# Rearranging the first stage of a transformer block on one core: conditioning vector in rows, a later gate load, fourteen extra products and a share of the normalisation on GpSimd

## The chip, the cores and the metric

The kernel runs on one core of a Trainium2 chip. A core has TensorE (matrix products; the profile's PE, with PEld for the loading of the stationary operand), VectorE (DVE), ScalarE (ACT), GpSimd (POOL), and SyncE (SP), which issues all DMAs of this kernel. Each engine works through its own instructions in order; semaphores tie the engines together. The metric is the device time of one execution in microseconds (us), as a median of several runs.

## The reference

The input x has 2048 tokens of 1024 channels. A vector c of 1024 numbers goes through silu and a 1024 x 6144 matrix and gives six modulation vectors.

```
mod = silu(c) @ w_mod              -> sa, ca, ga, sb, cb, gb
h = layernorm(x) * (1 + ca) + sa
x = x + ga * attention(h)          # 32 heads of 32, four segments of 512 tokens,
                                   # masked softmax inside a segment plus a running memory,
                                   # mixed by g = sigmoid(beta), one g per head
h = layernorm(x) * (1 + cb) + sb
x = x + gb * mixer(layernorm(h))   # W2 gelu(W1 .) across the tokens, 3584 hidden
```

## The kernel before, in words

**Stages.** First comes an opening of about 70 us: it loads x, makes the first two modulation vectors, normalises segment 0 and projects it. Attention over eight groups of four heads and four segments follows until about 1000 us, then the output projection and the two products of the token mixer, which TensorE fills until the end.

**Precision.** Operands of the large products are kept as two parts, a rounded one ("hi", made by a cast) and the rest ("lo", made by a subtraction); three products hi·hi, hi·lo and lo·hi stand for one. `split` makes both parts: for weights and for the pages of segment 0 ScalarE casts and VectorE subtracts; for the pages of segment 1 VectorE casts, and the subtraction goes to VectorE for odd and to GpSimd for even chunks. A "page" `h{seg}_{ct}` is one chunk of 128 channels by 512 tokens of the modulated, normalised input of a segment. Chunk ct's scale and shift (`saca`) come from two tiles `wm` of the modulation matrix, each multiplied by silu(c) and summed on VectorE (L285).

**The opening, step by step.** c arrives as 128 partitions x 8 (`csb`), silu is made on it, VectorE spreads it (`bc`), TensorE transposes that eight times, and ScalarE copies it out as `scb`, silu(c) on every partition. `norm_tiles` takes the statistics of a set of token tiles on VectorE, makes one over the deviation with Ln and Exp on ScalarE and four short VectorE steps, and then normalises each tile of 128 x 1024 with one ScalarE instruction (L222). `h_chunk` transposes the chunk of four tiles on TensorE (`hps`), applies scale and shift on ScalarE into `h32` (a ring of three buffers) and splits the result. `first_chunk` adds the chunk's products for head groups 0 and 1 (`nps` for keys and values at L182, `qps` for queries at L190). Then segment 1 goes the same way (its tiles are x4 to x7), and its pages feed the third item of the attention stage.

**Gate.** `gate` is sigmoid(beta), loaded by a DMA that reads the same 128 bytes for all 128 partitions. GpSimd multiplies it into eight masks (`bdg`, one product at L318 and one small copy at L321 for each head group), which the memory update of each group needs; the first such update is on VectorE at L429.

**Who sets the order.** The program is written as a stream of instructions. A planner at the end (`Order`) estimates what each instruction costs, walks the program forward and backward in a few passes, and pins the resulting order on every engine. TensorE's instructions count double before `COLD` (28000 ns of the planner's time). A GpSimd product of 128 elements a partition counts 551 ns in its table of costs (520 with a margin of 6%), a small copy 121 ns. These are the planner's figures, not measured ones.

Of the kernel before, what the change touches and what calls it, by code (L numbers as in the profile page):

```python
# [9 lines left out]
F32 = mybir.dt.float32  # L10
# [4 lines left out]
ALU = mybir.AluOpType  # L15
# [5 lines left out]
P = 128  # L21
# [23 lines left out]
def attention_and_mlp(ctx, tc, x, wq, wkv, wo, beta, w1, b1, w2, b2, c, wm_a, wm_b, out):  # L45
# [49 lines left out]
    G.memset(eps, EPS)  # L95

    csb = acst.tile([P, 2, NK], F32, name="csb")
    SY.dma_start(csb[:, 0], c)
    A.activation(csb[:, 1], csb[:, 0], AF.Exp, scale=-1.0)
    V.tensor_scalar_add(csb[:, 1], csb[:, 1], 1.0)  # L100
    V.reciprocal(csb[:, 1], csb[:, 1])
    sc = const.tile([P, NK], F32, name="sc")
    V.tensor_mul(sc, csb[:, 0], csb[:, 1])
# [102 lines left out]
    def norm_tiles(pool, ts):  # L206
        n = len(ts)
        mv = pool.tile([P, n, 4], F32, tag="mvs", bufs=2, name="mvs")
        for i, t in enumerate(ts):
            st = const.tile([P, 2, 6], F32, tag="st", bufs=4, name="st")  # L210
            for j in range(2):
                V.bn_stats(st[:, j], t[:, 512 * j:512 * j + 512])
            V.bn_aggr(mv[:, i, 0:2], st)
        m, v, r, e = (mv[:, :, j] for j in range(4))
        A.activation(r, v, AF.Ln, bias=eps)
        A.activation(r, r, AF.Exp, scale=-0.5)
        V.scalar_tensor_tensor(e, v, EPS, r, op0=ALU.add, op1=ALU.mult)
        V.scalar_tensor_tensor(e, e, -0.5, r, op0=ALU.mult, op1=ALU.mult)
        V.scalar_tensor_tensor(r, e, 1.5, r, op0=ALU.add, op1=ALU.mult)
        V.scalar_tensor_tensor(e, m, -1.0, r, op0=ALU.mult, op1=ALU.mult)  # L220
        for i, t in enumerate(ts):
            A.activation(t, t, AF.Identity, scale=mv[:, i, 2:3], bias=mv[:, i, 3:4])  # L222

    def h_chunk(pool, xs, seg, ct):
        ps = bank("s2", 2, f"hps{seg}_{ct}")
# [35 lines left out]
    bc = s1p.tile([P, NK, P], F32, name="bc")  # L261
    V.tensor_copy(bc, sc.unsqueeze(2).to_broadcast([P, NK, P]))
    for i in range(2):
        ps = bank("pj", 2, f"scps{i}")
        for j in range(4):
            T.transpose(ps[:, 128 * j:128 * j + 128], bc[:, 4 * i + j], ident)
        A.copy(scb[:, 512 * i:512 * i + 512], ps)
    first = [[bank("pj", 2, "nps0_0"), bank("pj", 2, "nps0_1"), bank("s1", 2, "qps0")],
             [bank("pv", 1, "nps1_0"), bank("ms", 1, "nps1_1"), bank("s1", 2, "qps1")]]
# [11 lines left out]
    for ct in range(NK):  # L281
        for part in range(2):
            wm = s1p.tile([P, D], F32, tag="wm", bufs=11, name=f"wm{ct}_{part}")
            SY.dma_start(wm, wm_a[part, ct])
            V.scalar_tensor_tensor(wm, wm, 1.0, scb, op0=ALU.mult, op1=ALU.mult, accum_out=saca[:, ct, part:part + 1])  # L285
        for kind, part, g in parts.get(ct, ()):
            split_part(g, kind, part, fetch_part(g, kind, part))
        V.tensor_scalar_add(saca[:, ct, 1:2], saca[:, ct, 1:2], 1.0)
        h_chunk(s1p, xs[0], 0, ct)
        if ct:  # L290
            for g in range(2):
                first_chunk(g, ct - 1)
# [3 lines left out]
    norm_tiles(s2p, xs[1])  # L296
    for ct in range(NK):
        h_chunk(s2p, xs[1], 1, ct)
    gate = top.tile([P, 3, H], F32, name="gate")
    SY.dma_start(gate[:, 0], bass.AP(tensor=beta.tensor, offset=beta.offset, ap=[[0, P], [1, H]]))  # L300
    A.activation(gate[:, 1], gate[:, 0], AF.Exp, scale=-1.0)
    V.tensor_scalar_add(gate[:, 1], gate[:, 1], 1.0)
    V.reciprocal(gate[:, 0], gate[:, 1])
    V.tensor_scalar(gate[:, 1], gate[:, 0], -1.0, 1.0, op0=ALU.mult, op1=ALU.add)
# [9 lines left out]
    skt = [[q.tile([98, 2, L], F32R, name=f"sk{i}_{h}") for h in range(4)] for i, q in enumerate(sk_)]  # L314
    for sk in skt[0] + skt[1]:
        G.memset(sk[96:98, 1].bitcast(F32), 1.0)
    for g in range(NG):
        G.tensor_tensor(bdg[:, g, 0:128].rearrange("p (h e) -> p h e", h=4),  # L318
                        bd[:, 0:128].rearrange("p (h e) -> p h e", h=4),
                        gate[:, 0, 4 * g:4 * g + 4].unsqueeze(2).to_broadcast([P, 4, 32]), op=ALU.mult)  # L320
        G.tensor_copy(bdg[:, g, 128:132], bd[:, 128:132])  # L321
# [635 lines left out]
LATEB = 3000.0  # L957
HOLD = 1000.0
EARLY = 60000.0
STAY = 3000.0  # L960
SLACK = 1.06
DMA_SPREAD = 7000.0
# [115 lines left out]
class Order:  # L1078
# [182 lines left out]
    def forward(self, key):  # L1261
# [44 lines left out]
                add(i)  # L1306
        while len(seq) < n:
            t, e, i = self.pick(free, heap, future, key)
            x = self.X[i]
            if x.opcode == "DMACopy" and size_of(x.outs[0]) > BULK and link - t - ISSUED > BACKLOG:  # L1310
                heapq.heappush(future[e], (link - ISSUED - BACKLOG, i))
# [159 lines left out]
```

## Time and profile before

| | |
|---|---|
| median of 3 runs | 2207.83 us (2205.8 to 2208.32) |
| the profiled execution | 2210.61 us, its span 2208.9 us |
| TensorE busy | 2162.7 us (98%) |
| VectorE, ScalarE, GpSimd busy | 1732.7, 1097.1, 725.7 us |
| TensorE idle in the first 20 us | 16 us |

The span runs from the first to the last instruction of the profiled execution. Busy times add up instructions; a busy TensorE is not one at full rate, so the length of single products is worth reading too.

### The profile page before, as it was taken

What the parts mean: (1) busy time and instruction counts of PE and PEld (TensorE: products, weight loads), DVE (VectorE), ACT (ScalarE), POOL (GpSimd) and SP (SyncE); (2) the same over time, 40 slices, a digit from 0 to 9 for tenths busy, and PEclk for the clock granted to TensorE, in tenths of its full rate; (3) what the DMA queues carried; (4) which work ended last, traced back from release to release, by engine and by line L of the source; (5) the groups of instructions that cost most, each with busy time, mean ns of one, the idle gap of its engine ahead of it and who ended that gap; (6) DMA issues with size and microseconds to landing.
All of it is one profiled execution on the core that took longest, in us unless ns stands there. A gap on an engine that the chain in (4) does not pass through costs nothing.

```text
span 2208.9 us, 38272 instructions
## 1 busy us (share of the span) xinstructions
PE 2162.7 (98%) x13738; PEld 1876.5 (85%) x13738; DVE 1732.7 (78%) x3818; ACT 1097.1 (50%) x2008; POOL 725.7 (33%) x827
## 2 busy tenths in 40 slices
PE   6999999999999999989999999999999999999999
PEld 6899998989988999878878888888888888888887
DVE  8777777867787756678997555898889787878787
ACT  5688787566666665653443333633334242424232
POOL 3376676476777755551001000043321000000000
PEclk9999999999999999999999999999999999999999
DMA  9666676796777644664467555775549241414134
GB/s 370 189 204 189 192 223 196 244 288 201 224 213 235 181 135 107 191 211 157 139 238 277 191 194 197 276 278 200 201 175 337 86 157 58 149 53 148 58 124 152
DMA packets 174897, 421.74 MB, mean 191 GB/s; under 512 B 17492, under 2 KB 71796, under 8 KB 165748
## 3 DMA queue, kind: packets, MB, share of 16 engines
q1 hardware_dynamic: 174708, 419.30, 57.9%
q8 instruction: 109, 1.79, 0.3%
q14 instruction: 80, 0.66, 0.1%
HBM read 242.00 MB, written 126.37 MB: 167 GB/s over the span
## 4 chain that ended last, share of the span: by engine, by line
PE 83%; DVE 7%; POOL 2%; DMA 2%; ACT 2%; issue 1%; SPq 0%; DVEq 0%; POOLq 0%; ACTq 0%
PE mx L787 46%; PE nps L182 13%; PE qps L190 6%; PE po L688 4%; PE pv L498 4%; POOL ph L484 2%; PE a L469 1%; PE sz L445 1%; PE sx L445 1%; PE rd L417 1%; PE up L427 1%; PE a L472 1%; PE a L475 1%; PE sy L445 1%; PE ops L513 1%
## 5 line engine op out<-in xcount | busy, mean ns | idle before, releaser
L787 PE MATMUL mx<-bU,sp 128*128 128x512 f32 x2352 | 533.7, 389 | 0.9 <-DVE bU L116 0.9
L787 PEld LDWEIGHTS mx<-bU,sp 128*128 128x128 f32 x2352 | 441.3, 188 | 93.2 <-DVE bU L116 1.3
L113 ACT CAST sp<-wr 128x384 fp32r<-128x384 f32 (+2 forms) x408 | 218.4, 545 | 474.3 <-PE mx L787 386.8
L182 PE MATMUL nps<-wv,h 128*128 128x256 f32 x3072 | 444.8, 284 | 0.8 <-POOL h L116 0.6
L787 PE MATMUL mx<-bA,sp 128*128 128x512 f32 x1764 | 433.5, 389 | 1.6 <-ACT cc L792 0.7
L484 POOL TENSOR_TENSOR ph<-p,ph 128x640 f16<-128x640 f32 x256 | 385.3, 1524 | 110.1 <-ACT ph L482 109.0
L182 PEld LDWEIGHTS nps<-wv,h 128*128 128x128 f32 x3072 | 405.6, 189 | 7.0 <-POOL h L116 0.8
L787 PEld LDWEIGHTS mx<-bA,sp 128*128 128x128 f32 x1764 | 330.4, 188 | 72.7 <-ACT cc L792 1.3
L116 DVE TENSOR_TENSOR sp<-wr,sp 128x384 fp32r<-128x384 f32 (+2 forms) x408 | 260.4, 646 | 60.6 <-ACT sp L113 60.1
L794 DVE TENSOR_TENSOR ac<-mx,ac 128x512 f32<-128x512 f32 x280 | 190.7, 688 | 94.6 <-PE mx L787 93.4
L190 PE MATMUL qps<-h,wq 128*128 128x512 f32 x768 | 198.7, 400 | 0.1
L482 ACT CAST ph<-p 128x1280 f16<-128x1280 f32 x128 | 161.4, 1261 | 52.5 <-POOL p L480 51.5
L688 PE MATMUL po<-wo,ots 128*128 128x512 f32 x768 | 182.4, 392 | 0.5 <-ACT mv L125 0.5
L480 POOL TENSOR_SCALAR_AFFINE_SELECT p<-p 128x256 f32<-128x256 f32 x256 | 117.6, 469 | 188.8 <-ACT p L477 94.8
L688 PEld LDWEIGHTS po<-wo,ots 128*128 128x128 f32 x768 | 143.6, 189 | 29.8 <-ACT mv L125 0.9
L190 PEld LDWEIGHTS qps<-h,wq 128*128 128x128 f32 x768 | 140.8, 190 | 29.7 <-PE sz L445 0.5
L787 PE MATMUL mx<-bB,sp 128*128 128x512 f32 x588 | 165.9, 389 | 0.0
L446 DVE CUSTOM_DVE_ANT_0 sx<-sx,mask 128x128 f32<-128x128 f32 (+1 forms) x256 | 110.9, 434 | 69.6 <-PE sx L445 68.9
L659 POOL TENSOR_TENSOR tu<-cc 128x512 f32<-128x512 f32 x14 | 19.1, 1364 | 399.5 <-DVE cc L923 372.1
L787 PEld LDWEIGHTS mx<-bB,sp 128*128 128x128 f32 x588 | 110.4, 188 | 23.0
L498 PE MATMUL pv<-vp,ph 128*128 128x97 bf16 (+1 forms) x2560 | 117.1, 200 | 1.7 <-DVE am L505 1.0
L794 DVE TENSOR_TENSOR cc<-mx,cc 128x512 f32<-128x512 f32 x140 | 95.2, 684 | 25.6 <-PE mx L787 22.0
(179 smaller groups left out, 3258.3 us busy)
## 6 DMA issues: line engine op xcount, KB each, us to landing
sk<-sg SPq DMA_DIRECT2D x384, 128.0 KB
wr<-in_w_dram SPq DMA_DIRECT2D x28, 1024.0 KB
wr<-in_w_dram SPq DMA_DIRECT2D x32, 768.0 KB
bstu<-ucd SPq DMA_DIRECT2D x28, 768.0 KB
wv<-wsp SPq DMA_DIRECT2D x36, 512.0 KB
wsp<-wv SPq DMA_DIRECT2D x32, 512.0 KB
rawm<-in_wm_b_dram SPq DMA_DIRECT2D x32, 512.0 KB
pcd<-cc SPq DMA_DIRECT2D x14, 1024.0 KB
```

The costliest lines, as they stand in the source:

```text
L113: A.copy(hi, src)
L116: lo_eng.tensor_tensor(lo, src, hi.bitcast(F32), op=ALU.subtract)
L182: T.matmul(ps[:, aa], h[:, j, 128 * tt:128 * tt + 128], wt[:, i, o:o + 256], start=(n == 0), stop=(n >= 6 * NK - 2), skip_group_check=True)
L190: T.matmul(ps, wt[:, i, o:o + 128], h[:, j], start=(k + n == 0), stop=(3 * k + n == 3 * NK - 1))
L446: V.tensor_tensor_reduce(o, o, mask[:, 384 - 128 * i:], 1.0, -3.0e38, op0=ALU.add, op1=ALU.max, accum_out=mx[:, h % 2, i:i + 1])
L480: G.affine_select(w, w, pattern=[[0, 2], [1, 128]], compare_op=ALU.is_ge, fill=0.0, base=0, channel_multiplier=-1)
L482: A.copy(ph[:, 0], p32)
L484: G.tensor_tensor(ph[:, 1, c], p32[:, c], ph[:, 0, c], op=ALU.subtract)
L498: T.matmul(pv[:, i, 0:w], ph[:, part, o:o + 128], d["vp"][:, j, h, 0:w], start=(n == 0), stop=(n == 19), skip_group_check=True)
L688: T.matmul(ps, os_[:, i, P * ct:P * ct + P], wop[ct, nh][:, j], start=(n == 0), stop=(n == 3 * NK - 1))
L787: T.matmul(ps, ops[q][:, i, P * k:P * k + P], b[:, j], start=(m == 0 and first), stop=(m == 3 * nk - 1), skip_group_check=True)
L794: V.tensor_tensor(d, ps, d, op=ALU.add)
```

## The change

The edits, in the order of the program:

- **c in rows.** c arrives as 8 partitions x 128 (`cr`). silu is made there, and eight products with a selection matrix (`sel`, made by GpSimd) spread it over the partitions, in place of the VectorE copy and eight transposes.
- **Gate later.** The gate's load and its four short steps move from before segment 1's pages to after them in the program, into the pool `late`; the load leaves the start of SP's queue.
- **Extra products.** Fourteen products of 128 x 512 read the first hi weights and write a PSUM bank that is cleared when its first real product starts. Their results are not used.
- **Norms on GpSimd.** In `norm_tiles` every second tile is normalised by GpSimd.
- **Planner.** During the first 30000 ns of its own time the planner may leave VectorE idle for up to 200 ns for an instruction that is due earlier by more than 200.

```diff
-    csb = acst.tile([P, 2, NK], F32, name="csb")   # and its DMA, exp, add, reciprocal, product
+    cr = s1p.tile([NK, 2, P], F32, name="cr")
+    SY.dma_start(cr[:, 0], c)
...
-            T.transpose(ps[:, 128 * j:128 * j + 128], bc[:, 4 * i + j], ident)
+            T.matmul(ps[:, 128 * j:128 * j + 128], sel[:, 4 * i + j], cr[:, 0], start=True, stop=True)
...
         for i, t in enumerate(ts):
-            A.activation(t, t, AF.Identity, scale=mv[:, i, 2:3], bias=mv[:, i, 3:4])
+            if i % 2:
+                G.tensor_scalar(t, t, mv[:, i, 2:3], mv[:, i, 3:4], op0=ALU.mult, op1=ALU.add)
+            else:
+                A.activation(t, t, AF.Identity, scale=mv[:, i, 2:3], bias=mv[:, i, 3:4])
...
+        for pg, n in (((W[0, 0]["v", 0], 8), (W[0, 0]["q", 0], 6)) if ct == 0 else ()):
+            for _ in range(n):
+                T.matmul(first[1][1], pg[:, 0, 0:128], pg[:, 0], start=True, stop=True)
...
-    gate = top.tile([P, 3, H], F32, name="gate")    # its DMA and steps, before the attention pools open
+    gate = b.tile([P, 3, H], F32, name="gate")      # the same lines, after them
...
+            soon = WAIT.get(e, 0.0) if t < SOON else 0.0      # WAIT: DVE 200, Activation 0; SOON 30000
+            if soon and future[e] and future[e][0][0] <= t + soon:
+                near = [(key[j], r, j) for r, j in future[e] if r <= t + soon]
+                k, r, j = min(near)
+                if k < key[i] - EAGER and r < t + self.C[i][0]:      # EAGER 200
+                    heapq.heappush(heap[e], (key[i], i))
+                    free[e] = r
+                    continue
```

Since the planner works from the whole program, every engine's order changes in the opening and, in small swaps, through the first quarter of TensorE's instructions; behind that the orders are the same. Three places matter below. Line numbers of the changed kernel differ from those of before.

TensorE at the start, before; `scps` is the spread silu(c), `hps_0` to `hps_2` the transposes of segment 0's first chunks, `nps_0` the first real product:

```order
L266 MATMUL scps_150<-ident,bc 128x128 x4
L227 MATMUL hps_0_219<-ident,x_134 128x128
L227 MATMUL hps_1_252<-ident,x_134 128x128
L227 MATMUL hps_0_219<-ident,x_136 128x128
L227 MATMUL hps_1_252<-ident,x_136 128x128
```

The same place in the changed kernel (L293 are the extra products):

```order
L269 MATMUL scps_151<-cr,sel 128x128 x4
L293 MATMUL nps_1_161<-wv_0_0_0_205 128x512 x8
L223 MATMUL hps_0_234<-ident,x_128 128x128
L223 MATMUL hps_0_234<-ident,x_130 128x128
L223 MATMUL hps_1_267<-ident,x_128 128x128
L223 MATMUL hps_1_267<-ident,x_130 128x128
L293 MATMUL nps_1_161<-wq_0_0_0_213 128x512 x2
```

The extra products now stand ahead of and between the transposes; four more follow before `hps_2`.

VectorE around the first lo part of a page (`h_0`), before; `saca` is a chunk's scale and shift:

```order
L285 SCALAR_TENSOR_TENSOR wm_0_292,saca<-wm_0_292,scb 128x1024
L288 TENSOR_SCALAR saca<-saca 128x1
L303 RECIPROCAL gate<-gate 128x32
L285 SCALAR_TENSOR_TENSOR wm_1_295,saca<-wm_1_295,scb 128x1024
L116 TENSOR_TENSOR h_0_226<-h_0_0_224,h_0_226 128x512
L288 TENSOR_SCALAR saca<-saca 128x1
L116 TENSOR_TENSOR h_1_259<-h_0_1_257,h_1_259 128x512
```

And in the changed kernel:

```order
L294 TENSOR_SCALAR saca<-saca 128x1
L109 TENSOR_TENSOR wv_1_0_0_252<-rawv_0_250,wv_1_0_0_252 128x512
L288 SCALAR_TENSOR_TENSOR wm_0_307,saca<-wm_0_307,scb 128x1024
L288 SCALAR_TENSOR_TENSOR wm_1_310,saca<-wm_1_310,scb 128x1024
L109 TENSOR_TENSOR h_0_241<-h_0_0_239,h_0_241 128x512
L294 TENSOR_SCALAR saca<-saca 128x1
L109 TENSOR_TENSOR h_1_274<-h_0_1_272,h_1_274 128x512
```

The first lo part still comes behind the same six `wm` sums; the gate's reciprocal has left, and one weight split (`wv_1`) has moved ahead of it.

GpSimd where segment 1's pages are made (`h_0`, `h_2`, `h_4`, `h_6` are the lo parts of the even pages), before; the masks `bdg` stand far ahead of this place:

```order
L316 MEMSET sk_2_760 2x512
L116 TENSOR_TENSOR h_0_662<-h_1_0_660,h_0_662 128x512
L116 TENSOR_TENSOR h_2_682<-h_1_2_680,h_2_682 128x512
L116 TENSOR_TENSOR h_4_702<-h_1_4_700,h_4_702 128x512
L354 MEMSET v_1_838 128x4x4
L116 TENSOR_TENSOR h_6_722<-h_1_6_720,h_6_722 128x512
```

And in the changed kernel:

```order
L216 TENSOR_SCALAR x_637<-x_637,mvs 128x1024
L216 TENSOR_SCALAR x_641<-x_641,mvs 128x1024
L323 TENSOR_TENSOR bdg<-bd,gate 128x128 x2
L109 TENSOR_TENSOR h_0_677<-h_1_0_675,h_0_677 128x512
L326 COPY bdg<-bd 128x4 x2
L323 TENSOR_TENSOR bdg<-bd,gate 128x128
L326 COPY bdg<-bd 128x4
L323 TENSOR_TENSOR bdg<-bd,gate 128x128
L326 COPY bdg<-bd 128x4
L323 TENSOR_TENSOR bdg<-bd,gate 128x128
L109 TENSOR_TENSOR h_2_697<-h_1_2_695,h_2_697 128x512
```

Two norms and all eight mask pairs now share GpSimd's queue with the four lo parts; one pair stands between `h_2` and `h_4`, and the rest of the eight stand ahead of `h_6`.

More of the change, by code (lines that the diff above doesn't have):

```diff
@@ L97, in attention_and_mlp @@
     csb = acst.tile([P, 2, NK], F32, name="csb")
[L98 to L103, printed above, removed]
     saca = acst.tile([P, NK, 2], F32, name="saca")
@@ L208, in norm_tiles @@
         mv = pool.tile([P, n, 4], F32, tag="mvs", bufs=2, name="mvs")
+        m, v, r, e = (mv[:, :, j] for j in range(4))
         for i, t in enumerate(ts):
@@ L213, in norm_tiles @@
             V.bn_aggr(mv[:, i, 0:2], st)
-        m, v, r, e = (mv[:, :, j] for j in range(4))
         A.activation(r, v, AF.Ln, bias=eps)
@@ L260, in attention_and_mlp @@
     xs = {0: [load_x(s1p, tt) for tt in range(4)]}
-    bc = s1p.tile([P, NK, P], F32, name="bc")
-    V.tensor_copy(bc, sc.unsqueeze(2).to_broadcast([P, NK, P]))
+    sel = s1p.tile([NK, NK, P], F32, name="sel")
+    G.memset(sel, 1.0)
+    G.affine_select(sel, sel, pattern=[[-1, NK], [0, P]], compare_op=ALU.is_equal, fill=0.0, base=0, channel_multiplier=1)
+    cr = s1p.tile([NK, 2, P], F32, name="cr")
+    SY.dma_start(cr[:, 0], c)
+    A.activation(cr[:, 1], cr[:, 0], AF.Exp, scale=-1.0)
+    V.tensor_scalar_add(cr[:, 1], cr[:, 1], 1.0)
+    V.reciprocal(cr[:, 1], cr[:, 1])
+    V.tensor_mul(cr[:, 0], cr[:, 0], cr[:, 1])
     for i in range(2):
@@ L298, in attention_and_mlp @@
         h_chunk(s2p, xs[1], 1, ct)
-    gate = top.tile([P, 3, H], F32, name="gate")
[L300 to L304, printed above, removed]
     left.__exit__(None, None, None)
@@ L316, in attention_and_mlp @@
         G.memset(sk[96:98, 1].bitcast(F32), 1.0)
+    gate = b.tile([P, 3, H], F32, name="gate")
+    SY.dma_start(gate[:, 0], bass.AP(tensor=beta.tensor, offset=beta.offset, ap=[[0, P], [1, H]]))
+    A.activation(gate[:, 1], gate[:, 0], AF.Exp, scale=-1.0)
+    V.tensor_scalar_add(gate[:, 1], gate[:, 1], 1.0)
+    V.reciprocal(gate[:, 0], gate[:, 1])
+    V.tensor_scalar(gate[:, 1], gate[:, 0], -1.0, 1.0, op0=ALU.mult, op1=ALU.add)
     for g in range(NG):
@@ L959 @@
 EARLY = 60000.0
+EAGER = 200.0
+WD, WA = 200.0, 0.0
+SOON = 30000.0
+WAIT = {"DVE": WD, "Activation": WA}
 STAY = 3000.0
@@ L1454 @@
         "b2": f("B_b2").reshape(NT, P).T,
-        "c": f("c").reshape(NK, P).T,
+        "c": f("c").reshape(NK, P),
         "wm_a": wm[:, :2 * D].T.reshape(2, NK, P, D),
```

## The prediction

> **What bounds the kernel now.** I read the page first, then busy time by stretch, then the timelines of TensorE, VectorE and GpSimd through the first 75 us.
>
> ```profile
> span 2208.9 us, 38272 instructions
> PE 2162.7 (98%) x13738; PEld 1876.5 (85%) x13738; DVE 1732.7 (78%) x3818; ACT 1097.1 (50%) x2008; POOL 725.7 (33%) x827
> ...
> PE 83%; DVE 7%; POOL 2%; DMA 2%; ACT 2%; issue 1%; SPq 0%; DVEq 0%; POOLq 0%; ACTq 0%
> ...
> core 0: us, PE busy (x) PEld busy (x) DVE busy (x) ACT busy (x) POOL busy (x), PEclk, DMA share, GB/s
> 0.00:10.00 10.00, 1.94 (x8) 1.57 (x8) 3.99 (x10) 3.17 (x6) 2.47 (x19) 1.00 0.68 230
> 10.00:20.00 10.00, 2.07 (x6) 0.87 (x6) 9.36 (x25) 6.89 (x11) 0.00 (x0) 1.00 1.03 415
> 20.00:30.00 10.00, 8.94 (x43) 7.97 (x44) 10.00 (x20) 7.45 (x13) 7.02 (x9) 1.00 1.02 409
> 30.00:40.00 10.00, 10.00 (x75) 9.35 (x74) 10.00 (x20) 3.83 (x6) 7.91 (x8) 1.00 1.03 408
> ```
>
> TensorE is busy for 98% of the span, so only what shortens its idle or slow time counts, and most of that lies in the first 22 us. There VectorE is the full engine (9.36 of 10 us, then all of it). The profiled execution took 2210.61 us, 1.7 more than its span and 2.8 more than the median, 2207.83. I work out a difference and add it to the median.
>
> TensorE's timeline, start and duration first:
>
> ```profile
> 6.30 1.94 PE L266 MATMUL scps<-ident,bc 128*128 128x128 f32 x8 [6.30 <-DVE bc L262]
> ...
> 25.05 1.91 PE L182 MATMUL nps<-wv,h 128*128 128x256 f32 x8
> ...
> 28.24 1.53 PE L182 MATMUL nps<-wv,h 128*128 128x256 f32 x12
> ...
> 71.92 0.74 PE L182 MATMUL nps<-wv,h 128*128 128x256 f32 x4 [0.63 <-POOL h L116]
> ```
>
> Eight products of 256 columns took 1.91 us at 25 us, twelve took 1.53 at 28: 0.24 against 0.13 each. So TensorE ran at half rate until about 27.5 us, although the granted clock of every stretch reads 1.00. From there it worked without a gap until 71.3 us, where it waited 0.63 us for GpSimd to finish page `h_6` of segment 1. These are the two places the change touches.
>
> **c in rows.** TensorE's spread takes 1.94 us now; if a product here costs two passes of a transpose, 3.9. The VectorE copy goes. All of it ends before anyone needs it:
>
> ```profile
> 8.28 0.59 ACT L267 COPY scb<-scps 128x512 f32<-128x512 f32 x1 [0.27 <-PE scps L266]
> ...
> 10.57 1.29 DVE L212 BATCH_NORM_STATS2 st<-x 128x6 f32<-128x512 f32 x2 [1.58 <-DMA x<-in_x_dram]
> ...
> 15.13 1.22 DVE L285 SCALAR_TENSOR_TENSOR wm<-wm,scb 128x1024 f32<-128x1024 f32 x1
> ```
>
> `scb` is ready at 8.9 us and first used at 15.13, so 6 us cover it. Ln and Exp stand behind those copies on ScalarE; a spread 2 us longer makes the first statistics wait until about 11, which uses up what an earlier x tile could give. Price 0.
>
> **The gate's load** leaves SP's queue at the start. While it and c came in, the rate fell:
>
> ```profile
> GB/s 0 0 115 224 374 363 284 115 161 181 302 383 421 421 426 410 415 426 426 421 404 404 426 393 415 426 382 415 426 393 415 415 415 404 404 415 404 404 421 399
> ```
>
> Each figure covers 0.75 us. Against 415, the eight figures from 374 to 383 lack 0.87 MB, about 2.1 us of the stream. VectorE waited 1.58 us for an x tile. Bounds: nothing, to 1.6 us earlier on VectorE. I take none, because of the norms below.
>
> **Norms on GpSimd.** ScalarE needs this for the first set, and for the second:
>
> ```profile
> 14.43 2.36 ACT L222 ACTIVATE x<-x,mvs 128x1024 f32<-128x1024 f32 x2
> ...
> 55.39 3.56 ACT L222 ACTIVATE x<-x,mvs 128x1024 f32<-128x1024 f32 x3
> ```
>
> That is 1.2 us a tile, so two tiles fewer per set free 2.4 us of ScalarE. No row shows this operation on GpSimd. GpSimd's forms, mean ns of one behind the comma:
>
> ```profile
> L480 POOL TENSOR_SCALAR_AFFINE_SELECT p<-p 128x256 f32<-128x256 f32 x256 | 117.6, 469 | 188.8 <-ACT p L477 94.8 <-ACT p L473 87.2 <-ACT mv L125 2.9
> L508 POOL TENSOR_TENSOR am<-am,red 128x128 f32<-128x128 f32 x96 | 56.8, 592 | 45.1 <-DVE red L505 39.1 <-PE sx L445 2.6 <-PE nps L182 1.5
> ...
> L318 POOL TENSOR_TENSOR bdg<-bd,gate 128x128 f32<-128x128 f32 x8 | 8.3, 1036 | 19.5 <-DVE gate L303 19.5
> L321 POOL COPY bdg<-bd 128x4 f32<-128x4 f32 x8 | 7.3, 915 | 0.0
> L116 POOL TENSOR_TENSOR h<-h,h 128x512 fp32r<-128x512 f32 x4 | 6.0, 1488 | 10.5 <-DVE h L115 10.5
> ```
>
> Four times the one-input form of 256 gives 1.9 us; a two-input form of 1024 would be twice 1488 ns, 3.0. I take 1.3, below both, because the one-input form has a fixed part. GpSimd was idle there, but the two engines get in each other's way:
>
> ```profile
> 61.25 0.43 DVE L115 CAST h<-h 128x512 fp32r<-128x512 f32 x1 [1.05 <-ACT h L229]
> 61.92 1.46 DVE L115 CAST h<-h 128x512 fp32r<-128x512 f32 x1 [0.25 <-ACT h L229]
> ...
> 61.82 1.28 POOL L116 TENSOR_TENSOR h<-h,h 128x512 fp32r<-128x512 f32 x1 [8.33 <-DVE h L115]
> ```
>
> The same cast takes 0.43 us alone and 1.46 while GpSimd's subtraction runs, and both end within 0.3 us of each other. So a GpSimd norm can hold VectorE up for its whole length, in a stretch where VectorE is full: 0 to 2.6 us for the two. Against it, the masks leave this stretch, where they slowed VectorE:
>
> ```profile
> 28.05 1.42 DVE L285 SCALAR_TENSOR_TENSOR wm<-wm,scb 128x1024 f32<-128x1024 f32 x1
> ...
> 23.83 0.88 DVE L116 TENSOR_TENSOR h<-h,h 128x512 fp32r<-128x512 f32 x1
> ```
>
> A `wm` sum took 1.42 beside them against 1.22, an h split 0.88 against 0.68 for a weight split; over some eight such pieces that is 1.5 us back. Loss and gain of VectorE cancel within 1.5 us.
>
> **The extra products.** A 512-column product takes twice a 256-column one, 0.48 us at half rate: 14 of them 6.7 us, from about 12 to 20 us, in TensorE's idle time. They wait for weight casts and stand ahead of the transposes; no real product is ready for its lo part then, so the cover holds, and without it the last four would cost 1.9 us. After them TensorE does some 1.5 us of hi·hi products of `h_0` and then waits for the lo part. In the order that part still stands behind six `wm` sums; it gains the gate's reciprocal (0.34 us) and loses one weight split (0.68 us):
>
> ```profile
> 22.48 0.34 DVE L303 RECIPROCAL gate<-gate 128x32 f32<-128x32 f32 x1
> ...
> 27.45 0.68 DVE L116 TENSOR_TENSOR wv<-rawv,wv 128x512 fp32r<-128x512 f32 x1
> ```
>
> Before, it ended at 24.7; now at about 24.9 (24.3 to 26.1). So TensorE idles some 3 us again just after it was warmed. One row shows what such a gap does:
>
> ```profile
> 940.95 0.63 PE L688 MATMUL po<-wo,ots 128*128 128x512 f32 x2
> ...
> 946.22 0.77 PE L469 MATMUL a<-sk 98*128 98x512 f32 x1 [2.87 <-DMA sk<-nt]
> ...
> 947.53 1.05 PE L688 MATMUL po<-wo,ots 128*128 128x512 f32 x2
> ...
> 949.64 1.15 PE L688 MATMUL po<-wo,ots 128*128 128x512 f32 x4
> ```
>
> After 2.87 us of idleness a pair took 1.05 instead of 0.63 us, and four took 1.15 again at 949.6: a gap of this size costs about half of 3.7 us, 1.9. [...]
>
> TensorE's way from there: of the 43.8 us that it worked from 27.5 to 71.3, all is left, and 1.2 us more (a few products and transposes that it had done by 27.5). From 24.9 that gives 69.9 at full rate, 71.8 with the slow start: about where it was, 71.3.
>
> **Gate and masks later, the term that decides.** The lo parts of pages 0, 2, 4, 6 of segment 1 now share GpSimd's queue with eight pairs of mask product and copy, and TensorE's third item waits for `h_6`. ScalarE waits too, since `h32` has three buffers and the later pages need the earlier lo parts done. The pairs start when the gate's reciprocal is there, behind the segment's statistics, two ScalarE norms instead of four, and a few short steps: I put that at 58 us (56.5 to 59.5; the old norms ended at 59). A pair took 1036 + 915 ns with VectorE full. In the new place VectorE is partly free:
>
> ```profile
> 23.00:38.00 15.00, 15.00 (x95) 13.95 (x94) 15.00 (x27) 8.18 (x14) 14.91 (x16) 1.00 1.03 408
> 58.00:72.00 14.00, 13.37 (x107) 12.55 (x106) 10.80 (x19) 11.70 (x23) 6.05 (x5) 1.00 0.96 268
> ```
>
> The masks' old place had VectorE busy for all of 15 us, the new one for 10.8 of 14, and about half of that on work of the kinds that got in the way above. GpSimd's nearest uncrowded row is the 592 ns product, and a copy of four elements should cost less than that: a pair costs 0.7 us at best, 1.95 at worst. I take 1.4, the middle, since about half of VectorE's time there collides. Eight pairs are 11.2 us, four lo parts at 1488 ns 6.0, together 17.2: `h_6` is ready at 75.2, against 71.9 before, 3.3 us later. TensorE has been standing since about 71.
>
> Some of that comes back, as other chains go on meanwhile and TensorE's later waits shrink:
>
> ```profile
> 74.53 0.33 PE L445 MATMUL sx<-sk 96*128 96x128 f32 x1 [0.38 <-DVE mx L446]
> ...
> 84.61 0.50 PE L469 MATMUL a<-sk 98*128 98x512 f32 x1 [0.72 <-DMA sk<-nt]
> ```
>
> With two shorter ones I give back 1.5 us of them. Behind that, to about 450 us, instructions only swap places; TensorE waits little there, and I allow 1.5 us either way. **Sum:** 3.3 - 1.5 = 1.8 us slower, 2209.6 us, no change that counts: 0.2% is 4.4 us, about what a measurement of this kernel can tell from no change. TensorE is not held by the slow first products or by the opening in this sum, since GpSimd's queue ends later than either.
>
> **The rivals.**
>
> *Faster: the opening's gain goes through.* If GpSimd is seldom in VectorE's way, a pair costs 0.7 and a lo part 1.28 us: 10.7 us from 57 makes `h_6` ready at 67.7, before TensorE wants it. If the x tiles also come 1.6 us earlier, `h_0`'s lo part ends at 23.3, the gap shrinks to 1.5 us and the clock stays up: TensorE reaches the place at 68.3 instead of 71.9, 3.6 us sooner, and with a later wait or two gone 5: 2202.8 us. For it: VectorE's 1.58 us wait and the rate that fell with the small loads; the idle GpSimd of the opening. Against it: the masks' order and their measured length. Chance of a gain above 0.2%: 0.17.
>
> *Slower: GpSimd's queue becomes the bound.* The masks collide with VectorE as they did at 23 to 38 us, 1.95 us a pair: 15.6 + 6.0 from 58 gives 79.6, 7.7 later, 1.5 of it given back: 6.2 slower, 2214.0 us. The point from which it decides is a pair of about 1.75 us, where `h_6` comes at 77.8 and the loss passes 4.4. For it: the eight measured pairs; the cast held for 1.03 us; and VectorE, held by GpSimd in turn, makes the casts for the next pages late. Against it: VectorE is idle for a quarter of that time. [...] Chance: 0.24.
>
> *The products do not warm TensorE, or warm it in vain.* This is the change not doing what it says. The transposes between 15.7 and 21 us did not raise the rate before, and the gap behind the products may undo it. TensorE would then reach `h_6` at 71.8, still ahead of GpSimd: the sum stays at 2209.6. It costs 1.9 us only in the faster rival. I hold it more likely than not, and it is inside the forecast's share.
>
> **How the numbers follow.** The forecast, within 0.2%, gets 0.59, the slower rival 0.24, the faster 0.17. Predicted: 2209.6. The range runs from the faster rival's 2202.8 to the slower one's 2214.0; beyond these ends lie the corners in which all bounds fall on one side, about 0.1 on each. The forecast's own range is 2203.4 to 2212.2.
>
> **What would show it.** Right: GpSimd's lo part of `h_6` ends past 73 us and TensorE's wait for it, 0.63 us now, grows to 3 or 4; mask pairs of 1.1 to 1.7 us; a hole of TensorE of about 3 us before the first lo product, and 512-column products still at 0.4 us or more behind it. The first real product starts near 20 instead of 22.5 us, without use. Wrong: no wait for `h_6`, pairs near 0.7 us, or `h_0`'s lo part well before 24 us; the forecast also falls if waits between 100 and 450 us change by more than 2 us.

## Result and the profile after

The changed kernel takes 2238.36 us (median of 4 runs, 2237.51 to 2241.27) against 2207.07 for the kernel before (4 runs, 2205.8 to 2208.32): a ratio of 1.0144, 95% interval 1.0127 to 1.0162. That is 31 us slower, where 1.8 were forecast, and far above the upper end of the range, 2214.0. The profiled execution took 2241.27 us with a span of 2239.6.

The page of the changed kernel, busy time of TensorE and the others, then the shares of the chain that ended last:

```profile
span 2239.6 us, 38318 instructions
PE 2200.0 (98%) x13760; PEld 1885.0 (84%) x13760; DVE 1731.8 (77%) x3817; ACT 1094.7 (49%) x2004; POOL 724.6 (32%) x833
...
PE 85%; DVE 7%; DMA 3%; ACT 2%; POOL 1%; issue 1%; SPq 0%; DVEq 0%; ACTq 0%; POOLq 0%
```

TensorE is busy 37 us longer than before (2162.7), with 22 instructions more, the 14 extra products and 8 of the spread. The time did not go into waiting; products got longer. Which ones, the groups by line say. The token mixer's products, kernel before, then after (busy us, mean ns of one):

```profile
L787 PE MATMUL mx<-bU,sp 128*128 128x512 f32 x2352 | 533.7, 389 | 0.9 <-DVE bU L116 0.9
L787 PE MATMUL mx<-bA,sp 128*128 128x512 f32 x1764 | 433.5, 389 | 1.6 <-ACT cc L792 0.7 <-DVE sp L116 0.6 <-ACT sp L113 0.2
L787 PE MATMUL mx<-bB,sp 128*128 128x512 f32 x588 | 165.9, 389 | 0.0
```

```profile
L792 PE MATMUL mx<-bU,sp 128*128 128x512 f32 x2352 | 549.2, 395 | 0.0
L792 PE MATMUL mx<-bA,sp 128*128 128x512 f32 x1764 | 444.2, 395 | 0.7 <-DVE sp L109 0.6 <-ACT sp L106 0.2
L792 PE MATMUL mx<-bB,sp 128*128 128x512 f32 x588 | 168.4, 393 | 0.0
```

The same 4704 products, in the same order, are busy 28.7 us longer. It is no stretch of slow clock (granted 1.00 from 1140 to 1680 and from 1700 to 2200 us in both) but every product, as TensorE's timeline inside the mixer shows, before and then after:

```profile
1301.10 0.84 PE L787 MATMUL mx<-bB,sp 128*128 128x512 f32 x3
1301.78 2.20 PE L787 MATMUL mx<-bA,sp 128*128 128x512 f32 x9
1303.82 0.84 PE L787 MATMUL mx<-bB,sp 128*128 128x512 f32 x3
```

```profile
1300.59 2.26 PE L792 MATMUL mx<-bA,sp 128*128 128x512 f32 x9
1302.69 0.85 PE L792 MATMUL mx<-bB,sp 128*128 128x512 f32 x3
1303.39 2.26 PE L792 MATMUL mx<-bA,sp 128*128 128x512 f32 x9
```

Twelve products took 2.72 us before (1301.10 to 1303.82) and take 2.80 now (1300.59 to 1303.39): 0.227 and 0.233 each. The views of the tile `mx` tell where the stage starts and ends (minimum, median and maximum ns, then first and last start):

```profile
L787 PE MATMUL mx<-bU,sp x2352: 387/389/499, 1669.9 to 2204.1; 128*128 128x512 f32 x196
L787 PE MATMUL mx<-bA,sp x1764: 387/389/500, 1133.7 to 1669.0; 128*128 128x512 f32 x196
```

```profile
L792 PE MATMUL mx<-bU,sp x2352: 388/394/505, 1686.0 to 2234.8; 128*128 128x512 f32 x196
L792 PE MATMUL mx<-bA,sp x1764: 389/396/502, 1137.4 to 1685.1; 128*128 128x512 f32 x196
```

The mixer starts 3.7 us later (1137.4 against 1133.7) and then takes 1097.4 instead of 1070.4 us: 27.0 of the 30.7 us between the two spans are made in a stage that the change does not touch.

What the change does touch there is the place of its data. The tile `sc`, 8 numbers or 32 bytes per partition, is gone from `const`, the first pool on the left side of SBUF, so the pools behind it on that side start 32 bytes lower. Three of them, `late`, `sk0` and `sk1` of the attention stage, start 352 bytes higher instead, since the 384 bytes of `gate` now lie ahead of them, and the tiles that `gate` had lain ahead of on the right side start 384 higher. In the built programs `sp` (the stationary operand of all mixer products) starts at byte 1728 before and 1696 after, `bB` at 30400 and 30368. `bA` and `bU` lie in another pool of the right side, which is laid out from the other end, and stay at 143296. The experiments test whether this is the cause.

### The profile page after: what moved, and what is told of

Its sections match the earlier page's. It is cut to its first block, busy times and chain, and to the rows that moved or that the text cites. A ratio compares the mean times of both kernels' runs of the same rounds, so it can differ in the third digit from the quotient of the medians.

```text
span 2239.6 us, 38318 instructions
## 1 busy us (share of the span) xinstructions
PE 2200.0 (98%) x13760; PEld 1885.0 (84%) x13760; DVE 1731.8 (77%) x3817; ACT 1094.7 (49%) x2004; POOL 724.6 (32%) x833
## 4 chain that ended last, share of the span: by engine, by line
PE 85%; DVE 7%; DMA 3%; ACT 2%; POOL 1%; issue 1%; SPq 0%; DVEq 0%; ACTq 0%; POOLq 0%
PE mx L792 49%; PE nps L175 13%; PE qps L183 6%; PE po L693 4%; PE pv L503 4%; PE a L474 1%; PE sz L450 1%; PE sx L450 1%; PE rd L422 1%; PE up L432 1%; DMA sk<-sg 1%; POOL ph L489 1%; PE a L477 1%; PE a L480 1%; DMA rawm<-in_wm_b_dram 1%
## 5 line engine op out<-in xcount | busy, mean ns | idle before, releaser
L792 PE MATMUL mx<-bU,sp 128*128 128x512 f32 x2352 | 549.2, 395 | 0.0
L792 PE MATMUL mx<-bA,sp 128*128 128x512 f32 x1764 | 444.2, 395 | 0.7 <-DVE sp L109 0.6
L792 PEld LDWEIGHTS mx<-bB,sp 128*128 128x128 f32 x588 | 110.4, 188 | 26.1
```

The source lines that it names most:

```text
L792: T.matmul(ps, ops[q][:, i, P * k:P * k + P], b[:, j], start=(m == 0 and first), stop=(m == 3 * nk - 1), skip_group_check=True)
```

## Experiments

### Is it the addresses?

Theory: where the operands of a mixer product lie decides its length. Rival: the changed orders, or what they leave behind (clock, traffic), slow the mixer. Two edits, one from each kernel.

In the changed kernel, 32 unused bytes at the place of `sc`:

```
-    eps = const.tile([P, 1], F32, name="eps")
+    eps = const.tile([P, 1], F32, name="eps"); const.tile([P, NK], F32, name="pad3")
```

> The changed kernel with an unused tile of 32 bytes in the pool `const`, where `sc` had been. Orders of all engines are those of the changed kernel; only addresses on the left side of SBUF move by 32 bytes, so that `sp`, `bB`, `ots`, `wo` and the h pages start at a multiple of 64 bytes again. Address theory: a mixer product takes 0.227 us as before instead of 0.2325, the loss of some 28 us goes, and about 2208 to 2211 us are left, the opening's own effect (forecast 2209.6). Rival, that the changed orders, the clock or the traffic of the opening slow the mixer: 2238 as the changed kernel, 0.2325 us a product. In between (2220 to 2230): both have a part.

Measured: 2211.39 us (10 runs), a ratio to before of 1.0012, interval 1.0002 to 1.0023. Its mixer:

```profile
L792 PE MATMUL mx<-bU,sp 128*128 128x512 f32 x2352 | 533.7, 389 | 0.8 <-DVE bU L109 0.8
L792 PE MATMUL mx<-bA,sp 128*128 128x512 f32 x1764 | 433.6, 389 | 1.7 <-DVE sp L109 1.1 <-ACT sp L106 0.5
L792 PE MATMUL mx<-bB,sp 128*128 128x512 f32 x588 | 165.9, 389 | 0.0
```

In the kernel before, the pool of `sc` alone:

```
-    sc = const.tile([P, NK], F32, name="sc")
+    sc = acst.tile([P, NK], F32, name="sc")
```

> The kernel before with one word changed: `sc` is taken from the pool `acst` in place of `const`. Nothing else of the change is in it, and every engine's order is that of before; the left side's pools start 32 bytes lower as in the changed kernel. Address theory: 4704 mixer products by 5.8 ns are 27 us, so 2234 to 2238 us. Rival (any part of the change that alters orders or work is the cause): 2207 as before.

Measured: 2242.48 us (4 runs), 1.0157 (1.0136 to 1.0178). Both fall as the theory says: 32 unused bytes take the loss away, and moving one tile of 32 bytes makes it without anything else of the change. The rival falls. That e2 lies above the 2238 us that I allowed is attention: its mixer starts at 1141.9 us, 8.2 later than before. That is more than single executions differ by: in before, e3, e4, e6, e7, e10 and e11, which all have the opening and attention of before, the mixer starts between 1130.2 and 1135.6 us (more below).

### Which operand, and what about its address?

All of these start from the kernel before, keep its orders, and put unused bytes into one or two of the mixer's pools:

```
e3  sp.tile([P, 8])  ahead of sp, yb.tile([P, 8])  ahead of bB     # sp +32, bB +64
e4  b3.tile([P, 8])  behind bA,   yb.tile([P, 8])  ahead of bB     # bA, bU -32, bB +32
e6  sp.tile([P, 8])  ahead of sp, b3.tile([P, 8])  behind bA       # sp +32, bB +32, bA, bU -32
e7  sp.tile([P, 16]) ahead of sp                                   # sp +64, bB +64
e10 sp.tile([P, 16]) ahead of sp, b3.tile([P, 16]) behind bA       # sp +64, bB +64, bA, bU -64
e11 sp.tile([P, 8])  ahead of sp, b3.tile([P, 56]) behind bA       # sp +32, bB +32, bA, bU -224
```

> The kernel before, with 32 unused bytes ahead of the pool `sp` and 32 behind it: only the mixer's stationary operand `sp` starts at 32 modulo 64; the moving operands `bA`, `bU` (unmoved) and `bB` (64 bytes on) stay at multiples of 64. Theory that the stationary operand's start counts: about 27 us longer, 2234. Rival that the moving operand or another tile (ots, wo, the pages) counts: 2207.

> The kernel before, with 32 unused bytes in `b3` and in `yb`: all moving operands of the mixer (`bA`, `bU`, `bB`) start at 32 modulo 64, `sp` stays at a multiple of 64. Theory that the stationary operand alone counts: 2207, the mixer's products 0.227 us each. Rival that a moving operand's start counts as well: 0.2325 us, 2234, or more, since in the changed kernel only `bB` (an eighth of the products) had a shifted moving operand.

> The kernel before with 32 unused bytes ahead of `sp` and 32 in `b3`, so that the stationary operand and all moving operands of the mixer start at 32 modulo 64; orders are those of before. One shifted alone cost 5.6 to 6.3 ns a product. Theory A, what counts is that the two differ in their place within 64 bytes: 0.227 us a product, 2207 to 2211. Theory B, each shifted operand costs by itself and the costs add: 0.239 us, 2265. Theory C, a product is held by whichever operand is shifted, once: 0.2325 us, 2236 to 2240. The products with `bB` in the changed kernel, where both operands were shifted, lie nearest to C.

> Control: the kernel before with 64 unused bytes ahead of `sp`, so that `sp` and `bB` move by 64 bytes and stay at multiples of 64. Theory (the place within 64 bytes counts): 0.227 us a product, 2207 to 2211. Rival (any other distance between the operands, or a boundary of 128 bytes or more, counts): another time, above or below.

> The kernel before with 64 bytes ahead of `sp` (so `sp` and `bB` go up by 64) and 64 bytes in `b3` (so `bA` and `bU` go down by 64); orders unchanged. What the runs show so far: products are fast where the starts of the two operands differ by a multiple of 256 bytes (the kernel before, e1, and `bB` in e6 and e7), slow where the remainder is 32, 64, 192 or 224. Here `sp` and `bA` differ by 128 modulo 256. Theory 128 (a line of 128 bytes counts): 0.227 us a product, about 2208. Theory 256: 0.2325 us with `bA` and `bU`, 2234 to 2237, `bB` at 390 ns.

> The kernel before with 32 bytes ahead of `sp` (so `sp` and `bB` go up by 32) and 224 bytes in `b3` (so `bA` and `bU` go down by 224): all operands of the mixer are moved, and their starts differ by a multiple of 256 again. Theory (the distance of the two operands modulo 256 or 128 counts, not the place of either): 0.227 us a product, 2207 to 2211. Rival (each operand has to stay at its own place, 64 modulo 128): 0.2325 us, 2234 to 2238.

Measured, with the starts of the operands modulo 256 bytes and the mean length of a product in each group:

| | sp / bA, bU / bB | apart: sp and bA, sp and bB | bU, bA, bB ns | us | ratio (interval) |
|---|---|---|---|---|---|
| before | 192 / 192 / 192 | 0, 0 | 389, 389, 389 | 2207.07 | |
| after | 160 / 192 / 160 | 32, 0 | 395, 395, 393 | 2238.36 | 1.0144 (1.0127 to 1.0162) |
| e3 | 224 / 192 / 0 | 32, 32 | 396, 395, 395 | 2238.32 | 1.0141 (1.0119 to 1.0164) |
| e4 | 192 / 160 / 224 | 32, 32 | 395, 395, 395 | 2239.03 | 1.0140 (1.0123 to 1.0157) |
| e6 | 224 / 160 / 224 | 64, 0 | 396, 395, 392 | 2235.85 | 1.0117 (1.0101 to 1.0132) |
| e7 | 0 / 192 / 0 | 64, 0 | 395, 395, 392 | 2234.76 | 1.0115 (1.0101 to 1.0129) |
| e10 | 0 / 128 / 0 | 128, 0 | 395, 394, 392 | 2234.28 | 1.0117 (1.0102 to 1.0132) |
| e11 | 224 / 224 / 224 | 0, 0 | 389, 389, 389 | 2209.96 | 1.0003 (0.9993 to 1.0012) |

I first took a boundary of 64 bytes on the stationary operand to be the cause. Both halves of that fell: the moving operands moved alone (e4) cost as much, and a move by 64 bytes, which was meant as a control (e7), cost nearly as much as one by 32. Theory C of e6 (2236 to 2240 us) came close to the time for a wrong reason. What is left is that these products are short where their two operands start at the same place within 256 bytes: 389 ns, against 394 to 396 for `bU` and `bA` where the starts are 32, 64 or 128 bytes apart. e11 tests that without either operand at its old place. The starts of `sp` and `bA` are 256 bytes apart modulo 512 before and 0 in e11, both fast (389 ns), and 128 apart in e10 is slow (395 and 394): that is why I count modulo 256. The groups of e11, and those of e10 for contrast:

```profile
L787 PE MATMUL mx<-bU,sp 128*128 128x512 f32 x2352 | 533.7, 389 | 0.0
L787 PE MATMUL mx<-bA,sp 128*128 128x512 f32 x1764 | 433.2, 389 | 2.2 <-ACT sp L113 1.2 <-ACT cc L792 0.7 <-DVE cc L794 0.2
L787 PE MATMUL mx<-bB,sp 128*128 128x512 f32 x588 | 165.9, 389 | 0.0
```

```profile
L787 PE MATMUL mx<-bU,sp 128*128 128x512 f32 x2352 | 548.7, 395 | 0.1
L787 PE MATMUL mx<-bA,sp 128*128 128x512 f32 x1764 | 441.3, 394 | 1.8 <-ACT sp L113 1.2 <-ACT cc L792 0.5
L787 PE MATMUL mx<-bB,sp 128*128 128x512 f32 x588 | 167.8, 392 | 0.0
```

The `bB` products of after, e6, e7 and e10 have their operands at the same place and still take 392 to 393 in the mean. They come in threes between nines of `bA`. Taken one by one from the traces, the first, second and third of a three take 392, 397 and 389 ns (medians) in after and 388, 397 and 389 in e10: the longest is the middle one, which has `bB` products on both sides. So the place of a product's own two operands is not all that counts, and being next to a `bA` product does not simply explain the rest; the cause stays open.

### Does it hold in attention, and is there a faster place?

In attention the weights `wv`, `wq` of most head groups lie 64 bytes modulo 256 away from the pages `h`, before and after alike (both moved by 32). e2 moved the pages alone. Unused bytes at the end of `acst` move the weights, and with them the other attention tiles of the left side:

```
-    bdg = acst.tile([P, NG, 132], F32, name="bdg")
+    bdg = acst.tile([P, NG, 132], F32, name="bdg"); acst.tile([P, 16], F32, name="pad3")    # e12, and e13 on e1
```

with 48 in place of 16 for e14 and 40 for e15.

> The kernel before with 64 unused bytes at the end of the pool `acst`: the weights `wv`, `wq` of head groups (128 modulo 256 before, the pages h 192) move up to 192, the same place as the pages; the attention tiles behind them move along; the mixer and all orders stay. Theory (the distance counts for every product): a `qps` product falls from 393 to 389 ns (median) and an `nps` product from 279 to about 274 to 276; some 3500 products by 3 to 5 ns are 10 to 18 us: 2190 to 2200. Rival (it counts for the mixer alone, since attention waits for other engines): 2207 to 2211.

> The changed kernel with its addresses put back (e1) and the same 64 bytes at the end of `acst`. By the theory 10 to 18 us below e1: 2192 to 2202, 2 to 3 us above the kernel before with the same 64 bytes, as e1 stood to it. If the change's opening is worth something once attention is faster, below it. Rival: as e1, 2210 to 2213.

> The kernel before with 192 unused bytes at the end of `acst`: the weights of head groups are 128 modulo 256 away from the pages h (64 before: `nps` 279, `qps` 393 ns median; 32 in e2: 281 and 396; 0 in e12: 283 and 389). Theory that products of 256 columns are best far from the place that is best for 512: `nps` 274 to 276, `qps` 394 to 396, so 3072 by 4 ns less 768 by 3 ns: about 10 us below before, 2197 to 2203. Rival, that 64 is as good as any and e12 was slower for another tile that moved along (sk, vp, v): `nps` 279 and above, 2208 to 2217.

> As e14 with 160 bytes: 96 modulo 256 away on the other side. Theory: `nps` between 275 and 279 ns, 2200 to 2207. Rival: 279 and above, 2208 to 2217.

| | apart | nps (256 columns) median, busy us | qps (512 columns) median, busy us | us | ratio (interval) |
|---|---|---|---|---|---|
| before | 64 | 279, 444.8 | 393, 198.7 | 2207.07 | |
| e2 | 32 | 281, 451.2 | 396, 199.6 | | (the mixer is slowed too) |
| e12 | 0 | 283, 453.9 | 389, 196.9 | 2216.09 | 1.0030 (1.0017 to 1.0044) |
| e14 | 128 | 281, 452.5 | 393, 199.2 | 2214.61 | 1.0034 (1.0022 to 1.0046) |
| e15 | 96 | 281, 454.9 | 397, 200.5 | 2219.47 | 1.0056 (1.0043 to 1.0068) |

The groups of before and of e12:

```profile
L182 PE MATMUL nps<-wv,h 128*128 128x256 f32 x3072 | 444.8, 284 | 0.8 <-POOL h L116 0.6 <-DVE h L116 0.2
L190 PE MATMUL qps<-h,wq 128*128 128x512 f32 x768 | 198.7, 400 | 0.1
```

```profile
L182 PE MATMUL nps<-wv,h 128*128 128x256 f32 x3072 | 453.9, 287 | 0.9 <-POOL h L116 0.6 <-DVE h L116 0.2
L190 PE MATMUL qps<-h,wq 128*128 128x512 f32 x768 | 196.9, 398 | 0.1
```

The 512-column `qps` products show the same: 389 ns at the same place, 393 at 64 and 128, 396 and 397 at 32 and 96. The 256-column products do not follow it: by their median they are longest at the same place (283 ns), by their busy time (453.9 us) as long there as at 96 and 128 apart (454.9 and 452.5). They are the more numerous: in e12 9.1 us are lost on them against 1.8 won. The same 64 bytes on e1 (e13) give 2215.75 us, 1.0031 (1.0018 to 1.0045), against 2192 to 2202 expected. My theory for these products fell with e14 and e15, which did not get below 281 ns. The kernel before already has the best of the five distances that ran; why 256 columns behave otherwise stays open, since `sk`, `vp`, `v` and `pk` moved as well, and no run moved the operands of `nps` alone. No kernel that I ran beats the kernel before.

### The opening by itself

e1 is the change with the addresses of the mixer and of the pages back where they were (the tiles that `gate` moved stay moved), so it measures the sum that the prediction made: 2209 by 0.0012 is 2.7 us slower (0.4 to 5.1), where 1.8 were forecast. Four kernels undo one part each, all from e1; the planner makes its orders anew for each of them.

```
e8   -((W[0, 0]["v", 0], 8), (W[0, 0]["q", 0], 6))   # no extra products
e9   gate, its DMA and four steps back before left.__exit__, in the pool top
e16  -if i % 2:   +if i > 9:                         # all norms on ScalarE
e17  -WD, WA = 200.0, 0.0   +WD, WA = 0.0, 0.0       # the planner idles no engine
```

> The changed kernel with its addresses put back (e1) and without the fourteen extra products; the orders are the planner's new ones. Theory (the prediction's): they warm TensorE in vain, since what follows waits for other engines: same as e1 within 2 us (2209 to 2213). Rival: they bring the 2 us that the half rate costs, so that without them 2213 to 2215.

> The changed kernel with its addresses put back (e1), and the gate's load and steps back at their old place, so that the masks stand early in GpSimd's queue again. The prediction's term: masks beside the pages of segment 1 cost 1.8 us net, so e1 minus 1.8: 2208 to 2210, and TensorE's waits between 70 and 90 us get shorter. Rival, what e1's trace shows (pairs of 0.9 us, no wait of TensorE for `h_6`): the masks cost nothing there and the early load takes from the x tiles again: same or up to 2 us longer, 2211 to 2214.

> The changed kernel with its addresses put back (e1), and all normalisations on ScalarE as before. If GpSimd's norms are what takes the opening's gain back (they take 1.5 to 2.1 us each and hold VectorE): 2 to 4 us below e1, 2207 to 2209. If they help, as extra products and late gate seem to: 2 to 6 us above e1, 2213 to 2217. If neither: 2210 to 2212.

> The changed kernel with its addresses put back (e1), and the planner's new idling of VectorE switched off. If the idling costs: 2207 to 2209. If it helps: 2213 to 2217. If neither: 2210 to 2212.

| | us | ratio to before (interval) |
|---|---|---|
| e1 | 2211.39 | 1.0012 (1.0002 to 1.0023) |
| e8, no extra products | 2216.86 | 1.0032 (1.0019 to 1.0044) |
| e9, gate early | 2215.72 | 1.0028 (1.0016 to 1.0039) |
| e16, norms on ScalarE | 2222.03 | 1.0064 (1.0052 to 1.0076) |
| e17, no idling | 2212.59 | 1.0028 (1.0018 to 1.0039) |

By the ratios each of the four is worse without its part: by 4.4 us for e8, 3.5 for e9, 11 for e16 and 3.5 for e17. Only for e16 are the intervals clear of each other, and its 11 us are more than the 2 to 6 that I allowed; the other three overlap e1's at their ends. Nor do their traces show where a loss would lie: their spans, 2212.2 us for e8, 2209.8 for e9 and 2210.0 for e17, are not longer than e1's, 2212.2. So it is shown that the norms on GpSimd help, with the order that goes with them; that the other three parts help is only likely. The measured times of e8 and e9 lie outside what their theories allowed (the products warm in vain; the masks cost 1.8 us in the new place), and none of the four kernels is faster than e1: no single part of these four is seen to keep e1 above before. Since the orders change with each, and in e9 the place of `gate` too, these are prices of a part with its new order. The rows of c were not tried alone.

## Why the prediction was wrong

**The step that failed** is the one behind the opening: "Behind that, to about 450 us, instructions only swap places", and with it the silence on everything later. I took an unchanged order of unchanged instructions for unchanged time. The diff showed `sc` leave `const`, and I priced only its instructions. The missing term of the sum is 4704 mixer products by 5.7 ns, 27 us, shown by e1 and e2 from both sides.

**The opening's sum** held in size (1.8 forecast, 2.7 measured by e1), but not by its deciding mechanism, so that its nearness is luck. Its first premise was too strong as well: of the 46 us that TensorE is idle before, 17 lie in the first 22 us, which is the largest piece but not most of it. Point by point, from the changed kernel's rows. TensorE's timeline:

```profile
6.40 3.75 PE L269 MATMUL scps<-cr,sel 8*128 8x128 f32 x16 [6.40 <-DVE cr L265]
12.23 3.78 PE L293 MATMUL nps<-wv 128*128 128x512 f32 x8 [2.09 <-ACT wv L106]
...
19.38 1.18 PE L293 MATMUL nps<-wq 128*128 128x512 f32 x4
...
20.93 0.74 PE L175 MATMUL nps<-wv,h 128*128 128x256 f32 x4
...
23.57 0.55 PE L223 MATMUL hps<-ident,x 128*128 128x128 f32 x3 [1.66 <-ACT h L225]
...
26.20 2.08 PE L175 MATMUL nps<-wv,h 128*128 128x256 f32 x8 [1.51 <-DVE saca L294]
...
85.67 0.47 PE L474 MATMUL a<-sk 98*128 98x512 f32 x1 [2.30 <-DMA sk<-nt]
```

*c in rows and gate's load: right.* The spread takes 3.75 us, close to the upper price that I gave. VectorE's wait of 1.58 us for an x tile is gone, and a wait of 1.15 us for ScalarE stands in its timeline instead: ScalarE's second copy waits 1.12 us for the spread, and Ln and Exp stand behind it. So the longer spread uses up what the earlier x tile gives, as forecast (ScalarE's row, then VectorE's):

```profile
10.18 0.59 ACT L270 COPY scb<-scps 128x512 f32<-128x512 f32 x1 [1.12 <-PE scps L269]
...
11.23 0.16 DVE L210 SCALAR_TENSOR_TENSOR mvs<-mvs 128x2 f32<-128x2 f32 x1 [1.15 <-ACT mvs L209]
```

*Extra products: right, with one limit.* They warm TensorE: 0.47 us each at 12 us, twice the 0.24 of a product of 256 columns as I took it, and 0.29 in the last four. Then the forecast hole before the first lo part comes, as two (1.66 and 1.51 us). The eight products behind them take 0.26 us each again, and the granted clock fell too (columns: stretch, its length, busy time of each engine, PEclk, DMA share, GB/s):

```profile
core 0: us, PE busy (x) PEld busy (x) DVE busy (x) ACT busy (x) POOL busy (x), PEclk, DMA share, GB/s
...
10.00:20.00 10.00, 7.19 (x22) 4.75 (x22) 8.49 (x22) 6.49 (x12) 3.59 (x2) 1.00 1.03 413
20.00:30.00 10.00, 6.83 (x35) 5.76 (x34) 9.97 (x21) 6.27 (x12) 0.00 (x0) 0.76 1.03 410
```

So in the changed kernel the products did warm in vain. Not quite so in e1, with the same orders. There the clock fell earlier (granted 0.97 in 0 to 20 us, 0.95 in 20 to 40), after holes of 0.73 and 0.83 us, and the last four extra products took 0.51 us each. It was back when the first real products came at 22.3 us, four in 0.72 us; the two holes behind them are 0.51 and 1.51 us, and the eight products after those took 0.15 us each. Here are e1's rows for that, and its first `a` product, to which I come below:

```profile
19.79 2.06 PE L293 MATMUL nps<-wq 128*128 128x512 f32 x4
...
26.37 1.21 PE L175 MATMUL nps<-wv,h 128*128 128x256 f32 x8 [1.51 <-DVE saca L294]
...
83.27 0.47 PE L474 MATMUL a<-sk 98*128 98x512 f32 x1 [2.07 <-DMA sk<-nt]
```

*Norms on GpSimd: 1.50 us in the mean against 1.3 taken*: 1.49 and 2.10 in the first set, where VectorE is nearly full, 1.2 each in the second (two in 2.39 us from 57.08). The fixed part that I took for the one-input form shows before the change in `ident` and `p`: 296 ns for 128 elements, 469 for 256. The one from 16.92 to 19.02 us overlaps a pair of weight splits on VectorE that took 2.09 us, where two alone take 1.36. That is 0.7 of the 1.2 us by which the lo part of `h_0` came later than my 24.9: it ended at 26.1, the late end of what I gave it:

```profile
18.08 2.09 DVE L109 TENSOR_TENSOR wq<-rawq,wq 128x512 fp32r<-128x512 f32 x2
...
25.46 0.68 DVE L109 TENSOR_TENSOR h<-h,h 128x512 fp32r<-128x512 f32 x1
```

*Gate and masks, the term that was to decide: wrong.* GpSimd's groups of the first 110 us, and its timeline:

```profile
L216 POOL TENSOR_SCALAR x<-x,mvs 128x1024 f32<-128x1024 f32 x4 | 6.0, 1499 | 16.4 <-DVE mvs L213 16.4
...
L323 POOL TENSOR_TENSOR bdg<-bd,gate 128x128 f32<-128x128 f32 x8 | 4.4, 557 | 1.7 <-DVE gate L320 1.7
...
L326 POOL COPY bdg<-bd 128x4 f32<-128x4 f32 x8 | 2.7, 340 | 0.0
```

```profile
16.92 2.10 POOL L216 TENSOR_SCALAR x<-x,mvs 128x1024 f32<-128x1024 f32 x1 [2.20 <-DVE mvs L213]
...
57.08 2.39 POOL L216 TENSOR_SCALAR x<-x,mvs 128x1024 f32<-128x1024 f32 x2 [6.42 <-DVE mvs L213]
61.19 0.76 POOL L323 TENSOR_TENSOR bdg<-bd,gate 128x128 f32<-128x128 f32 x2 [1.73 <-DVE gate L320]
...
71.80 1.48 POOL L109 TENSOR_TENSOR h<-h,h 128x512 fp32r<-128x512 f32 x1
```

A pair takes 0.90 us (557 + 340 ns) where I took 1.4, the nearer row being the uncrowded one. The pairs start at 61.2 instead of 58, and the two errors nearly cancel: `h_6` ends at 73.3, past 73 as forecast, by luck (in e1, with the same order, it ends at 71.1, ahead of the 71.9 of before). But TensorE does not wait for it: from 60 to 80 us it has other products without a gap. It waits later, 2.30 us at 85.67 for the DMA of `sk`, where before it waited 0.72 (none to 0.72 in the seven traces named above). In e1 that new wait is 2.07 us, and the clock fell behind it. TensorE from 80 to 100 us, before and then e1 (stretch, its length, busy time, PEclk, DMA share, GB/s):

```profile
80.00:100.00 20.00, 19.02 (x138) 1.00 0.46 143
```

```profile
80.00:100.00 20.00, 17.93 (x120) 0.91 0.50 160
```

That is 1.1 us less busy time and, at a mean clock of 0.91, about 1.8 us more lost. From 100 to 200 us TensorE is busy for 98.2 us in e1 against 99.2 to 99.3 in the seven, another 1 us. A single time does not tell a lead, since the first `a` product starts anywhere from 82.7 to 84.6 us in the seven (83.27 in e1). Counting TensorE's products that are still to come does, if roughly, as their order differs a little at first: with 13300 left e1 is ahead of all seven (79.8 us against 81.0 to 82.5), with 12000 left behind them (228.2 against 225.4 to 227.2), and with 10500 left, from where the order is the same, still behind (396.1 against 392.9 to 394.8). So the opening of e1 gains between 1.2 and 2.7 us, and it is lost again between 80 and 230 us. The mixer of e1 starts at 1136.7 us, 1.1 later than the latest of the seven; what adds to this behind 230 us is not settled.

**The rivals.** None of them had a mechanism outside the opening. "Slower: GpSimd's queue becomes the bound" got the side right and is refuted in its reason: pairs of 0.90 us, no wait for `h_6`. "Faster: the opening's gain goes through" is refuted too: there is a gain at 80 us in e1, though the lo part of `h_0` did not come early, and it did not go through. That the clock stays up through a gap of 1.5 us, as it took, shows in e1 (0.15 us a product behind holes of 0.51 and 1.51), not in the changed kernel (0.26 behind 1.66 and 1.51). The bounds of the range came only from stages that the diff named, which is why they were narrow in the wrong place.

## What to carry to other kernels

A tile that is removed or added moves what is laid out behind it (here by 32 bytes, `sp` from 1728 to 1696): before saying that an untouched stage costs the same, compare the start addresses of the operands of its products, and keep the place of a removed tile where they matter. The fp32r products of 512 columns in this kernel were shortest when both operands started at the same place within 256 bytes; the median of a product in an untouched stage tells (here 389 ns, or 392 to 397). A gain in an opening has to be followed to the first wait for something else: here a lead of 1.2 to 2.7 us was followed by a wait of 2.07 us for a transfer, and the clock fell on top.

## What was not expected of the hardware

- In these runs the length of an fp32r product of 128 x 512 changed with how far apart its two operands start, modulo 256 bytes: 0.227 us at the same place, 0.233 at 32, with medians of 389 against 392 to 397 ns. The `bB` products, at the same place between others that are not, are an exception that is not explained (392 to 393 ns in the mean). For 256 columns the same place had the longest median (283 against 279 to 281 ns), with other tiles moved along.
- The granted clock of TensorE fell behind two holes of 1.66 and 1.51 us in 4.3 us (0.76 in 20 to 30 us), behind one of 2.30 (0.91 in 80 to 100 us), and in e1 behind two of 0.73 and 0.83 in 2.7 us (0.97 in 0 to 20, 0.95 in 20 to 40 us) and one of 2.07 (0.91 in 80 to 100 us). It did not fall behind holes of 0.51 and 1.51 us in e1 (0.15 us for each of the eight products that follow), nor in e9 behind one of 2.48 us before the product at 85.65 (1.00 in 80 to 100 us). So the length of a hole alone does not decide in these runs.
